# Transposes of four attention steps as 64x64 TensorE tiles, among the tiled products of the step before

## Chip, core and metric

The kernel runs on one core of one Trainium2 chip, in one launch. The metric is the device time of an execution in microseconds (us), taken as the median over several runs; lower is better. The profile describes one of these executions.

## What is computed

The reference is a causal linear attention with decay over blocks of 64 positions, followed by a two-layer network with the tanh form of GELU. Four batches, eight heads, 768 positions, 64 values per head.

```python
for b in range(nb):                      # blocks of 64 positions
    qb, kb, vb = (q[:, :, sl], k[:, :, sl], v[:, :, sl])
    intra = np.einsum('bhic,bhjc->bhij', qb, kb) * Dmask[None]
    intra = np.einsum('bhij,bhjd->bhid', intra, vb)
    inter = np.einsum('bhid,bhde->bhie', qb * lam_pow[None], kv_state)
    out[:, :, sl] = intra + inter
    kb_dec = kb * rev_pow[None]
    kv_state = lam_block[None, :, None, None] * kv_state + np.einsum('bhsd,bhse->bhde', kb_dec, vb)
...
x = attn_out.transpose(0, 2, 1, 3).reshape(B * S, H * D)    # 3072 x 512
h = x @ w_in                                                # 512 x 2048
g = 0.5 * h * (1.0 + np.tanh(c * (h + 0.044715 * h * h * h)))
return g @ w_out                                            # 2048 x 512
```

## The kernel before

**Work units.** Attention is done in 24 steps (`NSTEP`). A step `s` is one stretch of 256 positions of one batch for four of the eight heads; two steps after each other (`s // 2`, the "superblock") cover all heads, and three superblocks make a batch, with a decayed state carried from one to the next. Everything that feeds TensorE is in fp16; PSUM sums are fp32.

**The pieces of a step.**
- `prep(s)`: VectorE scales q by the decay (line 225), ScalarE casts k (line 230), both into one tile `qk16`; POOL scales v (line 215). From step 9 (`FIRST_DMA_T`) on, `prep_qk` also issues a DMA transpose of q and k.
- `stage_t(s)`: for steps 0 to 8 it transposes q and k on TensorE: eight 128x128 transposes (line 246) into one PSUM bank `Tps`, which is then copied to SBUF as `qkT` by ScalarE (steps 1, 5, 6; line 253), by both (2 and 3; lines 250 and 251), or by VectorE (line 255).
- `scores(n)`: 16 matmuls in 64x64 tiles, `Sps` (line 275). `causal(n)` multiplies by the mask on VectorE, giving `PT` (line 284).
- `products(n, s)`: the state products of step n (`OK`, line 310) and the products of `PT` with v for the step before, s (line 324), both in 64x64 tiles; then, for s, two or four products of q with the carried state `u` over the full array (line 333). `x_out` has ScalarE copy the result to `xT` (line 352).
- `update(n, c)`: VectorE carries the state forward (`t`, lines 369 and 372), POOL masks it to `u` (line 379), which line 333 of the next step reads.

A 64x64 tile is a quarter of TensorE's array: a row half, which is the partition half that the operands lie on, and a column half, which is the partition half of PSUM that is written. The list `TILES` gives the order in which matmuls go round the four.

```python
TILES = [(0, 0), (1, 1), (0, 1), (1, 0)]
def half64(i):
    return slice(64 * i, 64 * i + 64)
```

**The network.** `queue_group(g)` puts the matmuls of the two layers for one group of superblocks into a list, `filler`, as small pieces: `mm1` (line 407, `Hps`, with a gelu on ScalarE at line 411), `mm2` (line 422, `O2ps`, copied by ScalarE at line 428), and for later groups `product` (line 476), which works with sums of weights and of activations. `fill(n)` issues the next n pieces. They stand between the pieces of attention, so that TensorE has work while other engines do theirs.

**Order.** `pin` keeps each engine's instructions in the order in which the code issues them. The order around the change is written out by hand at the end of the kernel. `R(n, s)` is `scores(n)`, `products(n, s)`, `causal(n)` and `update(n, 0)`; `U(n)` is `update(n, 1)`. Around steps 5 to 8 (lines 673 to 702):

```python
R(4, None); stage_t(5); U(4); prep(6); fill(2)
R(5, 4); stage_t(6); U(5); prep(7); fill(2)
R(6, 5); U(6); fill(1); prep(8); fill(1)
stage_t(7); fill(2)
R(7, 6); U(7); prep(9); fill(2)
# loop, n = 8:
stage_t(8); prep(10); fill(2); R(8, 7) ...
```

**PSUM.** `Tps`, the two banks of `OK` and the `Hps` and `O2ps` of the network all come from one pool, `ps_M`, of six banks; `Sps` has the other two. Which of the six a tile gets is settled when the kernel is built; a first write waits until the bank's last reader is done.

Of the kernel before, what the change touches and what calls it, by code (L numbers as in the profile page):

```python
# [9 lines left out]
FP16 = mybir.dt.float16  # L10
AF = mybir.ActivationFunctionType
# [4 lines left out]
def kernel(  # L16
# [10 lines left out]
    nc = tc.nc  # L27
    pin = tc.keep_in_program_order
    P = 128
# [9 lines left out]
    FIRST_DMA_T = 9  # L39
# [16 lines left out]
    ps_M = ctx.enter_context(tc.tile_pool(name="psM", bufs=6, space=PSUM))  # L56
# [98 lines left out]
    ident = const.tile([P, P], FP16)  # L155
# [40 lines left out]
    odd(halves[0])  # L196


    a16 = {}
    qkT = {}  # L200

# [18 lines left out]
    def prep_qk(s):  # L220
# [11 lines left out]
        if s >= FIRST_DMA_T:  # L232
# [2 lines left out]
                                            in_=tqk[:].rearrange("p a j h d -> p (a j h d)")))  # L235
            qkT[s] = o

    def stage_t(s):
        if s >= FIRST_DMA_T:
            return  # L240
        tq, tk = a16[s][:2]
        Tps = ps_M.tile([P, 2, 2, 2, P], FP16, tag="M", name="Tps")
        for i, t in enumerate((tq, tk)):
            for hp in range(2):
                for j in range(2):
                    pin(nc.tensor.transpose(Tps[:, i, j, hp, :], t[:, j, 2 * hp : 2 * hp + 2, :],  # L246
                                            ident[:]))
        o = qkp.tile([P, 2, 2, 2, P], FP16, tag="qkT", name=f"qkT_{s}")
        if s in (2, 3):
            pin(nc.scalar.activation(out=o[:, 0], in_=Tps[:, 0], func=AF.Copy))  # L250
            pin(nc.vector.tensor_copy(out=o[:, 1], in_=Tps[:, 1]))
        elif s in (1, 5, 6):
            pin(nc.scalar.activation(out=o[:], in_=Tps[:], func=AF.Copy))
        else:
            pin(nc.vector.tensor_copy(out=o[:], in_=Tps[:]))
        qkT[s] = o

    PTs = {}
    Kps = {}
    xT = {}  # L260
    state = {}
    TILES = [(0, 0), (1, 1), (0, 1), (1, 0)]

    def half64(i):
        return slice(64 * i, 64 * i + 64)

    Ss = {}

    def scores(n):
        o = qkT[n]  # L270
        Sps = ps_S.tile([P, 2, 2, 2, P], FP32, tag="S", name="Sps")
        for hp in range(2):
            for jk in range(2):
                for hl, c in TILES:
                    pin(nc.tensor.matmul(  # L275
                        Sps[half64(c), hl, hp, jk, :], o[half64(hl), 1, jk, hp, half64(c)],
                        o[half64(hl), 0, :, hp, half64(c)], start=True, stop=True,
                        skip_group_check=True))
        Ss[n] = Sps
# [10 lines left out]
    def products(n, s, banks=None, evacuate=True):  # L290


        OK, opened = banks or ([ps_M.tile([P, 512], FP32, tag="M", name=f"OK{c}")
                                for c in range(2)], set())

        def start(c, hl):
            if (c, hl) in opened:
                return False
            opened.add((c, hl))
            return True  # L300

        if n is not None:
            _, tk, tv = a16[n]
            last = (n // 2) % NSB == NSB - 1
            for jk in range(2):
                for hp in range(2):
                    for c, hl in TILES:
                        if c == 1 and last:
                            continue
                        pin(nc.tensor.matmul(  # L310
                            OK[c][half64(hl), 256 + hp * D : 256 + hp * D + D],
                            tk[half64(c), jk, 2 * hp + hl, :], tv[half64(c), jk, 2 * hp + hl, :],
                            start=start(c, hl), stop=(jk == 1), skip_group_check=True))
            Kps[n] = OK
        if s is None:
            return OK, opened
        sbg, half = divmod(s, 2)
        o = qkT.pop(s)
        PT = PTs.pop(s)
        _, _, tv = a16.pop(s)  # L320
        for hp in range(2):
            for jk in range(2):
                for c, hl in TILES:
                    pin(nc.tensor.matmul(  # L324
                        OK[c][half64(hl), hp * P : hp * P + P], tv[half64(c), jk, 2 * hp + hl, :],
                        PT[half64(c), hl, hp, jk, :], start=start(c, hl), stop=False,
                        skip_group_check=True))
        for c in range(2):
            if c == 0 and sbg % NSB == 0:
                continue  # L330
            u = us.pop((s, 0) if c else (s - 2, 1))
            for hp in range(2):
                pin(nc.tensor.matmul(OK[c][:, hp * P : hp * P + P], u[:, hp].rearrange("p l d -> p (l d)"),  # L333
                                     o[:, 0, :, hp, half64(c)], start=False, stop=True,
                                     skip_group_check=True))
        if evacuate:
            x_out(s, OK)
        return OK, opened

    def x_out(s, OK, second=None):  # L340
        sbg, half = divmod(s, 2)
        g, i = group_of[sbg]
        if g not in xT:
            xT[g] = xtp.tile([P, 2, len(groups[g]), 2, SB], FP16, tag="xT", name=f"xT_{g}")
        dst = xT[g][:, half, i]
        for c in range(2):
            d = dst[:, :, c * P : (c + 1) * P].rearrange("p hp (t j) -> p hp j t", j=2)
            o = OK[c][:, 0:256].rearrange("p (hp j t) -> p hp j t", hp=2, j=2)
            if c == 1 and second is not None:
                pin(second.tensor_copy(out=d, in_=o))  # L350
            else:
                pin(nc.scalar.activation(out=d, in_=o, func=AF.Copy))  # L352
# [237 lines left out]
    def R(n, s):  # L590
        if n is not None:
            scores(n)
        products(n, s)
        if n is not None:
            causal(n)
        if s is not None and s % 2 == 1:
            g, i = group_of[s // 2]
            if i == len(groups[g]) - 1 and g > 0:
                queue_group(g)
        if n is not None:  # L600
            update(n, 0)
# [5 lines left out]
    idle(9)  # L607
    prep(0)
    stage_t(0)
    idle(1)  # L610
    square(5)
# [3 lines left out]
    idle(2)  # L615
    R(0, None)
    stage_t(1)
    idle(5)
    U(0)
    prep(2)  # L620
    scores(1)
    products(1, 0)
    causal(1)
    idle(1)
    stage_t(2)
    prep_qk(3)
    update(1, 0)
    update(1, 1, "t")
    idle(3)
    scores(2)  # L630
    products(2, None)
    update(2, 0)
    causal(2)
# [109 lines left out]
```

## Time and profile before

| | |
|---|---|
| Time, median of 4 runs | 205.51 us |
| The four runs | 204.77, 204.85, 206.16, 206.18 us |
| The profiled execution: time, span of its instructions | 204.85 us, 203.1 us |
| TensorE busy, share of the span | 195.8 us, 96% |
| VectorE, ScalarE, POOL busy | 145.0, 108.1, 70.1 us |
| Transposes of steps 5 to 8 on TensorE | 32, first at 42.5 us, last at 55.9 us |
| One such transpose | 219 ns from start to end |
| Granted TensorE clock | 1.00 |

In the profile PE is TensorE's matmuls and PEld its weight loads, DVE is VectorE, ACT is ScalarE. "L246" is line 246 of the kernel, and a row names the tile that is written and the ones that are read. A matmul's duration includes the time that it takes to pass through the array, and matmuls follow each other at a closer distance than that; what each costs in a row of equal ones is read from the distance of their starts, or from the chain, which gives each piece its own share of the time.

### The profile page before, as it was taken

To read this page: it belongs to the slowest core of one execution; us is meant where nothing else is said; L and a number is where in the kernel's file an instruction comes from. 1 tells how busy PE (TensorE), PEld (TensorE's weight loads), DVE (VectorE), ACT (ScalarE), POOL (GpSimd) and SP (SyncE) were. 2 spreads that over 40 slices of the span, in tenths; PEclk is the share of its full clock that TensorE was granted. 3 is DMA by queue.
4 is the path that set the end of the run, shared out by engine and by line. 5 is a ranking of instruction groups with operands and counts; after the bars stand their busy time and mean duration, and the time that the engine had idled before them with its cause. 6 is when DMAs were issued, how large, how long until landed. Compare 5 with 4: busy or idle time off the path is not lost.

```text
span 203.1 us, 5595 instructions
## 1 busy us (share of the span) xinstructions
PE 195.8 (96%) x2325; PEld 127.7 (63%) x2325; DVE 145.0 (71%) x275; ACT 108.1 (53%) x204; POOL 70.1 (35%) x80
## 2 busy tenths in 40 slices
PE   7789999999999999999999999999999999999993
PEld 2456544456875788644688554788554788545882
DVE  4897728777699998929997728996739773136652
ACT  3365778375882573477632477641576431666210
POOL 4695133646586851336135404315412101000000
PEclk9999999999999999999999999999999999999999
DMA  5999999999999999896659992648330003300014
GB/s 157 301 322 391 385 386 377 294 290 326 339 257 230 292 245 147 217 286 165 69 159 235 233 269 80 152 109 134 94 91 0 3 0 103 108 0 0 3 47 160
DMA packets 63937, 37.85 MB, mean 186 GB/s; under 512 B 17576, under 2 KB 59048, under 8 KB 63912
## 3 DMA queue, kind: packets, MB, share of 16 engines
q1 hardware_dynamic: 63616, 37.23, 71.7%
q8 instruction: 18, 0.29, 0.6%
q10 hardware_dynamic: 296, 0.26, 0.4%
q14 instruction: 7, 0.06, 0.1%
HBM read 27.26 MB, written 6.29 MB: 165 GB/s over the span
## 4 chain that ended last, share of the span: by engine, by line
PE 91%; DVE 3%; DMA 1%; POOL 1%; ACT 1%; issue 1%; DVEq 0%
PE Hps L407 37%; PE O2ps L422 10%; PE MB L476 8%; PE MA L476 7%; PE MD L476 7%; PE MC L476 4%; PE Sps L275 4%; PE Hps L522 3%; PE OK L333 3%; PE OK L324 3%; PE Tps L246 2%; DMA lam_in<-in_lam_dram 1%; PE OK L310 1%; DVE PT L284 1%; POOL dq L174 1%
## 5 line engine op out<-in xcount | busy, mean ns | idle before, releaser
L407 PE MATMUL Hps<-xT,w_in 128*128 128x512 f16 (+1 forms) x416 | 79.1, 346 | 0.0
L411 ACT ACTIVATE gT<-Hps 128x512 f16<-128x512 f32 x88 | 52.4, 596 | 22.9 <-PE Hps L407 22.0
L407 PEld LDWEIGHTS <-w_in 128*128 128x128 f16 x416 | 40.3, 98 | 33.5
L379 POOL TENSOR_TENSOR u<-t,lumask 128x256 f16<-128x256 f32 x40 | 31.3, 790 | 79.9 <-DVE t L372 53.1
L452 DVE TENSOR_TENSOR gs<-gT 128x512 f16<-128x512 f16 (+1 forms) x70 | 36.6, 586 | 10.8 <-ACT gT L411 10.6
L284 DVE TENSOR_TENSOR PT<-Sps,mask 128x1024 f16<-128x1024 f32 x24 | 29.2, 1216 | 16.9 <-PE Sps L275 16.8
L476 PEld LDWEIGHTS <-gs 128*128 128x128 f16 x360 | 34.9, 98 | 4.0
L215 POOL TENSOR_TENSOR v<-v,dv 128x512 f16<-128x512 f32 x24 | 29.2, 1220 | 4.4 <-PE O2ps L422 1.8
L352 ACT ACTIVATE xT<-OK 128x256 f16<-128x256 f32 x47 | 18.1, 453 | 19.5 <-PE OK L333 15.9
L422 PE MATMUL O2ps<-w_out,gT 128*128 128x512 f16 x96 | 21.9, 379 | 0.0
L225 DVE TENSOR_TENSOR qk<-q,dq 128x512 f16<-128x512 f32 x23 | 19.2, 835 | 0.0
L230 ACT ACTIVATE qk<-k 128x512 f16<-128x512 f32 x24 | 15.0, 624 | 7.9 <-DMA k<-in_k_dram 7.9
L483 ACT ACTIVATE m<-MB 128x512 f32<-128x512 f32 x9 | 5.4, 597 | 25.4 <-PE MB L476 25.4
L476 PE MATMUL MA<-w_sum,gT 128*128 128x256 f16 x144 | 17.5, 273 | 0.1
L476 PE MATMUL MD<-w_sum,gs 128*128 128x256 f16 x136 | 17.5, 273 | 0.0
L476 PE MATMUL MB<-w_out,gs 128*128 128x256 f16 x144 | 17.2, 273 | 0.0
L476 PEld LDWEIGHTS <-gT 128*128 128x128 f16 x144 | 14.0, 98 | 2.8 <-ACT gT L411 0.3
L422 PEld LDWEIGHTS <-gT 128*128 128x128 f16 x96 | 9.2, 98 | 9.9
L487 DVE TENSOR_TENSOR o<-MA,m 128x512 f32<-128x512 f32 x9 | 6.2, 689 | 12.7 <-ACT m L483 12.7
L372 DVE SCALAR_TENSOR_TENSOR t<-t,lamu,OK 128x64 f32<-128x64 f32 x64 | 14.6, 273 | 0.7
L275 PEld LDWEIGHTS <-qkT 64*64 64x64 f16 x384 | 6.1, 106 | 8.5 <-issue 4.4
L123 DVE TENSOR_TENSOR w_sum<-wo,wo 128x1024 f16<-128x1024 f32 x6 | 7.9, 1363 | 4.2 <-DMA wo<-in_moe_w_out_dram 4.2
(59 smaller groups left out, 167.9 us busy)
## 6 DMA issues: line engine op xcount, KB each, us to landing
q<-in_q_dram SPq DMA_DIRECT2D x24, 256.0 KB, 4.8
k<-in_k_dram SPq DMA_DIRECT2D x24, 256.0 KB, 4.8
v<-in_v_dram SPq DMA_DIRECT2D x24, 256.0 KB, 4.9
out_dram<-o SPq DMA_DIRECT2D x22, 256.0 KB, 4.3
wo<-in_moe_w_out_dram SPq DMA_DIRECT2D x4, 1024.0 KB, 9.4
wi<-in_moe_w_in_dram SPq DMA_DIRECT2D x4, 512.0 KB, 7.4
wi<-in_moe_w_in_dram SPq DMA_DIRECT2D x2, 1024.0 KB, 13.0
out_dram<-o SPq DMA_DIRECT2D x2, 128.0 KB, 1.9
```

The source lines that it names most:

```text
L215: pin(nc.gpsimd.tensor_tensor(wide(tv[:]), ld32[s][2][:], decay(dv, s), ALU.mult))
L225: pin(q_eng.tensor_tensor(wide(tq), q32[:], decay(dq, s), ALU.mult))
L230: pin(nc.scalar.activation(out=wide(tk), in_=k32[:], func=AF.Copy))
L284: pin(nc.vector.tensor_tensor(t[:].rearrange("p a b c d -> p (a b) (c d)"), Ss.pop(n)[:].rearrange("p a b c d -> p (a b) (c d)"), mask[:]. ...
L352: pin(nc.scalar.activation(out=d, in_=o, func=AF.Copy))
L372: pin(nc.vector.scalar_tensor_tensor(t[:, hp, :], state[half][:, hp, :], lamu[:, 2 * half + hp : 2 * half + hp + 1], K[:, hp, :], ALU.mult ...
L379: pin(nc.gpsimd.tensor_tensor(u[:], state[half][:].unsqueeze(2).to_broadcast([P, 2, 2, D]), lumask[:, 2 * half : 2 * half + 2, :].unsqueez ...
L407: pin(nc.tensor.matmul(by_block(Hps[:, i, :]), w_in16[:, c, f * P : (f + 1) * P], x(c), start=(c == 0), stop=(c == NC - 1)))
L411: pin(nc.scalar.activation(out=dst, in_=Hps[:], func=AF.Gelu_apprx_tanh))
L422: pin(nc.tensor.matmul(O2[tau][0][:], gT[:, f % HF, f // HF, tau * P : (tau + 1) * P], w_out16[:, f, :], start=(n == 0), stop=(n == NF - 1)))
L452: pin(nc.vector.tensor_tensor(gsum[m][:, i, :], block(T0, F0, i), block(T1, F1, i), op))
L476: pin(nc.tensor.matmul(dst, lhsT, rhs, start=(i == 0), stop=(i == HF - 1), skip_group_check=True))
```

## The change

The transposes of steps 5 to 8 (`TILED_T`) leave `stage_t`. They are issued inside `products` of the step before, after the tiled products and ahead of the full-array products with `u` (for step 5, whose preceding `products` has no such part, at its end). Each of the eight 128x128 transposes becomes four of 64x64, one on each tile, 32 a step. They are written to two PSUM banks, one for each row half, in place of one. `stage_t` keeps its place and now only copies: two copies of half the size, one from each bank, by ScalarE for steps 5 and 6 and by VectorE for steps 7 and 8. Steps 0 to 4 go as before, and so do the steps from 9 on. `TILES` and `half64` move up unchanged.

```diff
+    TILED_T = range(5, FIRST_DMA_T)
+    Tps = {}
+
+    def transposes(s):
+        tq, tk = a16[s][:2]
+        if s not in TILED_T:
...
+            Tps[s] = t
+            return
+        ts = [ps_M.tile([P, 2, 2, 2, 64], FP16, tag="M", name=f"Tps{c}") for c in range(2)]
+        for i, src in enumerate((tq, tk)):
+            for hp in range(2):
+                for j in range(2):
+                    for c, hl in TILES:
+                        pin(nc.tensor.transpose(ts[c][half64(hl), i, j, hp, :],
+                                                src[half64(c), j, 2 * hp + hl, :],
+                                                ident[half64(c), half64(c)]))
+        Tps[s] = ts
+
     def stage_t(s):
         if s >= FIRST_DMA_T:
             return
-        tq, tk = a16[s][:2]
-        Tps = ps_M.tile([P, 2, 2, 2, P], FP16, tag="M", name="Tps")
-        for i, t in enumerate((tq, tk)):
-            for hp in range(2):
-                for j in range(2):
-                    pin(nc.tensor.transpose(Tps[:, i, j, hp, :], t[:, j, 2 * hp : 2 * hp + 2, :],
-                                            ident[:]))
+        if s not in TILED_T:
+            transposes(s)
+        t = Tps.pop(s)
         o = qkp.tile([P, 2, 2, 2, P], FP16, tag="qkT", name=f"qkT_{s}")
...
-        elif s in (1, 5, 6):
-            pin(nc.scalar.activation(out=o[:], in_=Tps[:], func=AF.Copy))
         else:
-            pin(nc.vector.tensor_copy(out=o[:], in_=Tps[:]))
+            for c in range(2) if s in TILED_T else (None,):
+                src, dst = (t[:], o[:]) if c is None else (
+                    t[c][:].rearrange("p i j h t -> p (i j h) t"),
+                    o[:, :, :, :, half64(c)].rearrange("p i j h t -> p (i j h) t"))
+                if s in (1, 5, 6):
+                    pin(nc.scalar.activation(out=dst, in_=src, func=AF.Copy))
+                else:
+                    pin(nc.vector.tensor_copy(out=dst, in_=src))
         qkT[s] = o
...
         if s is None:
+            if n + 1 in TILED_T:
+                transposes(n + 1)
             return OK, opened
...
+        if n is not None and n + 1 in TILED_T:
+            transposes(n + 1)
         for c in range(2):
             if c == 0 and sbg % NSB == 0:
                 continue
             u = us.pop((s, 0) if c else (s - 2, 1))
```

More of the change, by code (lines that the diff above doesn't have):

```diff
@@ L196, with half64 @@
     odd(halves[0])
+    TILES = [(0, 0), (1, 1), (0, 1), (1, 0)]
+    def half64(i):
+        return slice(64 * i, 64 * i + 64)
     a16 = {}
@@ L236, in prep_qk @@
             qkT[s] = o
+    TILED_T = range(5, FIRST_DMA_T)
[3 more added lines that the diff above has]
+        if s not in TILED_T:
+            t = ps_M.tile([P, 2, 2, 2, P], FP16, tag="M", name="Tps")
+            for i, src in enumerate((tq, tk)):
+                for hp in range(2):
+                    for j in range(2):
+                        pin(nc.tensor.transpose(t[:, i, j, hp, :], src[:, j, 2 * hp : 2 * hp + 2, :],
+                                                ident[:]))
+            Tps[s] = t
+            return
+        ts = [ps_M.tile([P, 2, 2, 2, 64], FP16, tag="M", name=f"Tps{c}") for c in range(2)]
+        for i, src in enumerate((tq, tk)):
+            for hp in range(2):
+                for j in range(2):
+                    for c, hl in TILES:
[3 more added lines that the diff above has]
+        Tps[s] = ts
     def stage_t(s):
@@ L240, in stage_t @@
             return
-        tq, tk = a16[s][:2]
-        Tps = ps_M.tile([P, 2, 2, 2, P], FP16, tag="M", name="Tps")
-        for i, t in enumerate((tq, tk)):
-            for hp in range(2):
-                for j in range(2):
-                    pin(nc.tensor.transpose(Tps[:, i, j, hp, :], t[:, j, 2 * hp : 2 * hp + 2, :],
-                                            ident[:]))
+        if s not in TILED_T:
+            transposes(s)
+        t = Tps.pop(s)
         o = qkp.tile([P, 2, 2, 2, P], FP16, tag="qkT", name=f"qkT_{s}")
         if s in (2, 3):
-            pin(nc.scalar.activation(out=o[:, 0], in_=Tps[:, 0], func=AF.Copy))
-            pin(nc.vector.tensor_copy(out=o[:, 1], in_=Tps[:, 1]))
-        elif s in (1, 5, 6):
-            pin(nc.scalar.activation(out=o[:], in_=Tps[:], func=AF.Copy))
-        else:
-            pin(nc.vector.tensor_copy(out=o[:], in_=Tps[:]))
+            pin(nc.scalar.activation(out=o[:, 0], in_=t[:, 0], func=AF.Copy))
+            pin(nc.vector.tensor_copy(out=o[:, 1], in_=t[:, 1]))
+        else:
+            for c in range(2) if s in TILED_T else (None,):
[6 more added lines that the diff above has]
+                    pin(nc.vector.tensor_copy(out=dst, in_=src))
         qkT[s] = o
@@ L261 @@
     state = {}
-    TILES = [(0, 0), (1, 1), (0, 1), (1, 0)]
-    def half64(i):
-        return slice(64 * i, 64 * i + 64)
     Ss = {}
```

## The prediction

> **What bounds the kernel now.** I read the page first: the busy times of the engines, the span in forty slices, and the shares of the chain that ended last.
>
> ```profile
> PE 195.8 (96%) x2325; PEld 127.7 (63%) x2325; DVE 145.0 (71%) x275; ACT 108.1 (53%) x204; POOL 70.1 (35%) x80
> PE   7789999999999999999999999999999999999993
> PEclk9999999999999999999999999999999999999999
> PE 91%; DVE 3%; DMA 1%; POOL 1%; ACT 1%; issue 1%; DVEq 0%
> ```
>
> TensorE is busy from the fourth slice to the last but one at full granted clock, and the chain is 91% TensorE. Steps 5 to 8 lie at 42 to 59 us, where nothing else bounds. Next I read TensorE's list of waits.
>
> ```profile
> PE idle L584 <- DVE ones L146: 1.5, 1, 1.5
> PE Tps L246 <- POOL dq L174: 0.6, 1, 0.6
> PE Sps L275 <- DVE qkT L251: 0.5, 1, 0.5
> PE OK L324 <- DVE PT L284: 0.4, 1, 0.4
> ```
>
> These waits all fall into the first 17 us. From there on TensorE does one thing after another, so what is taken from its sequence shortens the span one for one, unless the shorter sequence catches up with another engine. Third, the chain in order of time around the change (start, time on the chain, piece):
>
> ```profile
> 42.46 0.12 PE OK L310 x8
> 42.59 0.55 PE Tps L246 x8
> ...
> 45.89 0.45 PE Tps L246 x8
> 46.33 1.73 PE O2ps L422 x8
> 48.06 0.35 PE Sps L275 x16
> 48.41 0.12 PE OK L310 x16
> 48.53 0.23 PE OK L324 x16
> 48.76 0.33 PE OK L333 x4
> ...
> 50.83 0.45 PE Tps L246 x8
> ...
> 55.68 0.45 PE Tps L246 x8
> 56.13 1.75 PE Hps L407 x16
> ```
>
> Every piece of one step can be read here. L246 is the full-array transposes of steps 5, 6, 7 and 8. L275, L310 and L324 are products in 64x64 tiles; L333, L407 and L422 use the full array.
>
> **The change part by part.** *Removed:* four times eight full-array transposes. Three cost 0.45 us each, 56 ns apiece. The first costs 0.55, because it stands behind tiled work and carries the switch from tiles to the full array, 0.10; step 4's products have no L333 behind them. That switch stays, and is paid by the L422 that now follows. So 4 x 0.45 = 1.80 us leave.
>
> *Added:* four times 32 transposes of 64x64, at the end of the tiled products of the step before. The trace has no tiled transpose. The nearest row is L310: the same tile, the same 64 moving columns, a 64-column weight load from the same qk tile before each, and two output banks split by row tile, as the change does. Its 16 take 0.12 us, 7.5 ns each, so 32 take 0.24. That is my value: 4 x 0.24 = 0.96 us. Bounds from the rows: below, the work can't be less than nothing, so the gain is at most the 1.80 removed; above, the tiles don't overlap at all for transposes. Then each 64-column transpose takes half of L246's 56 ns, 28 ns, and 32 take 0.90 us, 3.58 in all, a loss of 1.8. I stay at the L310 row, since only the transpose flag and the fp16 output differ from it.
>
> *Switches of mode:* none is added or saved. The new transposes stand behind L324 (L310 in step 4) and ahead of L333, inside a stretch that is tiled already. In the old place they stood between full-array work. The sum on TensorE is 0.96 - 1.80 = -0.84 us.
>
> A rule speaks against this. The Trainium skill, TensorE: Matmul & The Clock Gate, section on the 56 ns that aren't 53.3, says that matmul starts are never closer than about 25 ns however few the columns. By it 32 transposes would take an estimated 0.80 us, and the change would lose 4 x 0.35 = 1.4 us. The L310 row, at 7.5 ns from start to start over four tiles, says that this floor doesn't hold across tiles, and I go by the row.
>
> **Who might now be late.** The program's order is kept on each engine, so I went through every wait that moved.
>
> Inputs: the transposes of a step now need its q and k earlier. They stand on TensorE ahead of L333 and all filler, so a late k would stop everything. For step 6 q is done at 44.73 and k at 44.78, and the transposes come at about 45.15. For step 7 k is the closest.
>
> ```profile
> 45.81 0.77 ACT L352 ACTIVATE xT<-OK 128x256 f16<-128x256 f32 x2 [0.55 <-PE OK L333]
> 46.43 1.02 ACT L253 ACTIVATE qkT<-Tps 128x1024 f16<-128x1024 f16 x1
> 47.35 0.62 ACT L230 ACTIVATE qk<-k 128x512 f16<-128x512 f32 x1
> ```
>
> That is the timeline of ScalarE (start, time). In step 5's products L333 comes after the new 0.24, but 0.21 was saved before it, so it starts about 0.04 later, and so do these three. The evacuation of step 6 becomes two halves. A half is 0.60 us (L250, 597 ns), the second starting about 0.48 after the first as the two-in-a-row L428 do, so both take 1.08 instead of 1.02. It ends at about 47.57, and k of step 7 at 48.07. TensorE wants that qkT for scores(6) at 47.99 - 2 x 0.21 = 47.57: the half microsecond of slack that stood there is used up, and I book a wait of 0.03 us (0 to 0.15). The first k transpose of step 7 comes at about 48.30, after 48.07.
>
> Steps 7 and 8 are evacuated by VectorE, two halves of 0.42 (L251, 420 ns) for one of 0.69, 0.15 us more for each. After step 7's VectorE was idle for 1.42 us, waiting for scores. For step 8 the halves need no wait for a TensorE that just finished, and end near 56.3; scores(8) come near 57.0. If that cover were gone, each would cost at most its 0.15.
>
> L333 itself waits for u from POOL: u of step 4 is done at 45.19 and of step 5 at 47.94, ahead of 45.55 and 48.6. No DMA is issued or moved by the edit; loads, output stores and DMA transposes keep their place in SP's queue.
>
> Banks: the pool has six, and two instead of one are held from the products of step n until the evacuation ahead of step n+1's scores. In the built program the banks that transposes 5 to 8 and the products behind them take were last read, at the latest, by the gelu of the first L407 block (ends 52.25, wanted at about 52.9) and by the evacuation of the transposes before (about 47.5, wanted at 48.2). None is late. From step 9 on the sequence of tenants is the old one with other numbers. If one of these came late, it would cost the missing part of one 0.6 us activation.
>
> Sum: -0.84 + 0.03 = -0.81 us, say 0.8. All TensorE work after 58 us moves up by that, and since its only other gap there is 0.2 us at 76 us, it stays. The profiled run has a span of 203.1 in a time of 204.85: 202.3 and 204.05 after. The runs shown are 204.77, 204.85, 206.16 and 206.18, with median 205.51; the profiled run is one of the low pair. I forecast the median: 205.51 - 0.8 = 204.7 us.
>
> **The rivals.** (a) *Slower: the tiles don't overlap for transposes.* Place: the 32 transposes of each step. Price: 0.90 - 0.45 = 0.45 us a step, 1.8 us over four; scores(6) come later by more than qkT of step 6 does, so no wait adds to it. Time 207.3. It decides from 14 ns per transpose up (0.45 / 32), where the gain is gone; over 1% needs 30 ns, for example if each transpose also drained its tile. For it: no row shows a tiled transpose, nor two kinds of pass overlapping. Against it: L310 and L275 overlap fourfold, and L246 stands beside L333 and L407 with no gap, so the transpose flag alone costs no drain.
>
> (b) *The gain is eaten by waits.* ScalarE's chain of x, qkT and k in step 6 comes late by more than I booked, for example 0.5 us by one more activation ahead of it, and one bank comes late. Time 205.3. For it: the slack is nearly nothing. Against it: it occurs once, in step 6; from step 7 on there is half a microsecond or more.
>
> (c) *The transposes vanish under their neighbours.* If the tiled passes fill gaps between L310 and L324, up to 1.8 us is saved: 203.7, still under 1%. Against it: the tiled stretch has no gap to fill but its switches.
>
> **How the numbers follow.** Forecast 0.62, at 204.7; (b) 0.15; (a) 0.18, about half of it above 1%, with still slower transposes in its tail; (c) 0.05. One per cent is 2.05 us, about what a measurement of this kernel can tell from no change. The forecast, (b) and (c) lie within it; faster by over 1% needs more than the whole 1.80 that is removed, and can come only from the scatter of the runs or something that I don't see: 0.06. Slower by over 1%: 0.13, from the upper half of (a) and its tail. Within: 0.81. The likeliest case alone spans 203.9 to 205.4, since runs differ by 1.4 among themselves. The range reaches from (c) with some scatter, 203.3, to just short of (a), 206.8.
>
> **What would show it.** Right: each step's transposes stand on the chain with 0.24 us in place of 0.45, behind L324 and ahead of L333; the old places show filler following filler; scores(8), at 57.80 before, start near 57.0; TensorE's waits after 21 us show at most one for qkT of step 6, below 0.15. Wrong: tiled transposes with 28 ns or more from start to start mean rival (a); a TensorE wait for ScalarE's qkT or for k at 47 to 49 us means (b); scores(8) early but the span unchanged means that the gain was given back after 58 us, which I have excluded.

## The result, and the profile after

| | before | changed |
|---|---|---|
| Median time | 205.18 us (58 runs, 204.76 to 206.43) | 206.22 us (37 runs, 204.66 to 207.59) |
| Ratio | | 1.0038, 95% interval 1.0024 to 1.0053 |
| Profiled execution: time, span | 204.85, 203.1 us | 206.31, 204.5 us |
| TensorE instructions (weight loads and matmuls) | 4650 | 4842 |

The change made the kernel slower by 0.4%; the ratio is that of the means, the medians differ by 0.5%. The forecast was 204.7 us, 0.4% below the median of 205.51 that it started from. First the page of the changed kernel: the busy times, the fetches of instructions over DMA, and the shares of the chain that ended last.

```profile
PE 194.6 (95%) x2421; PEld 126.9 (62%) x2421; DVE 145.3 (71%) x277; ACT 108.2 (53%) x206; POOL 70.0 (34%) x80
q8 instruction: 19, 0.31, 0.7%
PE 89%; DVE 4%; issue 2%; DMA 1%; POOL 1%; ACT 1%; DVEq 0%
```

TensorE's busy time fell by 1.2 us and the span grew by 1.4. The share called "issue", time for which the profile shows no cause, went from 1% to 2%. The instruction row of the page before was:

```profile
q8 instruction: 18, 0.29, 0.6%
```

TensorE's list of waits from 20 us to 200 us was empty before. Now it reads:

```profile
PE Tps L263 <- issue: 1.4, 1, 1.4
PE Hps L437 <- issue: 0.5, 1, 0.5
```

The chain in order of time shows where they lie (L301, L336, L352, L363, L437 and L452 are the old L275, L310, L324, L333, L407 and L422; L263 is the tiled transposes):

```profile
48.14 0.23 PE OK L352 x16
48.36 0.18 PE Tps L263 x22
48.54 1.37 issue
49.91 0.28 PE Tps L263 x10
50.19 0.33 PE OK L363 x4
...
54.48 0.23 PE OK L352 x16
54.70 0.28 PE Tps L263 x32
54.98 0.22 PE OK L363 x2
55.20 0.44 PE Hps L437 x4
55.63 0.47 issue
56.11 3.22 PE Hps L437 x28
```

Step 8's 32 tiled transposes cost 0.28 us, against 0.45 for eight full ones. So the tiles overlap. But in step 7 TensorE stops for 1.4 us behind the 22nd transpose, with neither q nor k nor a bank beginning there, and once more in the middle of a row of filler matmuls that wait for nothing.

**What stops it.** The page's instruction queue q8 carried 18 packets before and 19 now, each of 16 KB. 4842 instructions in 0.31 MB are 64 bytes each, so a packet is a block of 256. The weight loads (PEld) around the two stops:

```profile
48.12 0.31 PEld L263 LDWEIGHTS <-qk 64*64 64x64 f16 x23
49.91 0.17 PEld L263 LDWEIGHTS <-qk 64*64 64x64 f16 x9 [1.48 <-issue]
54.98 0.48 PEld L437 LDWEIGHTS <-w_in 128*128 128x128 f16 x5
56.11 0.97 PEld L437 LDWEIGHTS <-w_in 128*128 128x128 f16 x9 [0.65 <-issue]
```

Each matmul has its weight load ahead of it, so the n-th weight load of the trace is number 2n - 1 of TensorE's stream and the n-th matmul number 2n. The first weight load behind the first stop is number 1217, the first behind the second 1473 (matmuls 1216 and 1472 are recorded as starting with them): the stops are 256 instructions apart, the length of a block. The trace's packet records show the two fetches; the first packet of a profile is taken as the block behind number 449, the next as that behind 705, and so on. The first ran from 47.25 to 48.44 us, and TensorE, whose last matmul had started at 48.35, went on at 49.91. The second ran from 53.82 to 54.85; TensorE's last matmul had started at 55.36, and it went on at 56.11. From start to start, beyond the usual spacing, the two stops are 1.56 and 0.64 us.

The Trainium skill, Runtime: NRT & Kernel Launch, section Instruction fetch mechanics, describes the same: instructions reach an engine in 16 KB blocks of 256, each fetched by the sequencer's own DMA while it works through the one before, and crossing an edge is mostly hidden. The blocks agree with the packets here. "Mostly hidden" agrees with the other edges of this profile, at which TensorE doesn't stop, and not with these two, at 1.56 and 0.64 us.

**The balance.** scores(8) began at 57.80 us before and at 59.25 now, 1.45 later:

```profile
57.80 0.42 PE L275 MATMUL Sps<-qkT 64*64 64x128 f16 x16
59.25 0.42 PE L301 MATMUL Sps<-qkT 64*64 64x128 f16 x16
```

The two stops are 2.20; without them scores(8) would be 0.75 earlier. Forecast was 0.81. From there on the two traces run alike, to spans that differ by 1.4.

*Theory F* (supply): a block of 256 instructions is used up faster than the next arrives. The change adds 48 TensorE instructions a step (32 transposes for 8, each with its weight load) where they were densest already. From its first matmul to its last ahead of the edge, the block ahead of 1217 took 7.2 us before and 3.4 now, the one ahead of 1473 8.2 and 5.5. *Theory W* (the rival): the early transposes wait for data or a bank, and the profile fails to name it.

### The profile page after: what moved, and what is told of

It reads as the page before. It is cut to its first block, busy times and chain, and to the rows that moved or that the text cites. A ratio compares the mean times of both kernels' runs of the same rounds, so it can differ in the third digit from the quotient of the medians.

```text
span 204.5 us, 5790 instructions
## 1 busy us (share of the span) xinstructions
PE 194.6 (95%) x2421; PEld 126.9 (62%) x2421; DVE 145.3 (71%) x277; ACT 108.2 (53%) x206; POOL 70.0 (34%) x80
## 4 chain that ended last, share of the span: by engine, by line
PE 89%; DVE 4%; issue 2%; DMA 1%; POOL 1%; ACT 1%; DVEq 0%
PE Hps L437 37%; PE O2ps L452 10%; PE MB L506 8%; PE MA L506 7%; PE MD L506 7%; PE MC L506 4%; PE Sps L301 4%; PE Hps L552 3%; PE OK L363 3%; PE OK L352 3%; DMA lam_in<-in_lam_dram 1%; PE OK L336 1%; DVE PT L310 1%; POOL dq L174 1%; PE Tps L254 1%
## 5 line engine op out<-in xcount | busy, mean ns | idle before, releaser
L437 PE MATMUL Hps<-xT,w_in 128*128 128x512 f16 (+1 forms) x416 | 78.9, 346 | 0.5 <-issue 0.5
L437 PEld LDWEIGHTS <-w_in 128*128 128x128 f16 x416 | 40.3, 98 | 34.1 <-issue 0.6
L310 DVE TENSOR_TENSOR PT<-Sps,mask 128x1024 f16<-128x1024 f32 x24 | 29.2, 1216 | 16.7 <-PE Sps L301 16.7
L452 PE MATMUL O2ps<-w_out,gT 128*128 128x512 f16 x96 | 21.9, 379 | 0.0
L230 DVE TENSOR_TENSOR qk<-q,dq 128x512 f16<-128x512 f32 x23 | 19.2, 837 | 0.0
L235 ACT ACTIVATE qk<-k 128x512 f16<-128x512 f32 x24 | 15.0, 625 | 7.3 <-DMA k<-in_k_dram 7.3
L452 PEld LDWEIGHTS <-gT 128*128 128x128 f16 x96 | 9.1, 98 | 10.0
L301 PEld LDWEIGHTS <-qkT 64*64 64x64 f16 x384 | 6.2, 106 | 8.5 <-issue 4.2
```

What stands on the lines that cost most here:

```text
L230: pin(q_eng.tensor_tensor(wide(tq), q32[:], decay(dq, s), ALU.mult))
L235: pin(nc.scalar.activation(out=wide(tk), in_=k32[:], func=AF.Copy))
L310: pin(nc.vector.tensor_tensor(t[:].rearrange("p a b c d -> p (a b) (c d)"), Ss.pop(n)[:].rearrange("p a b c d -> p (a b) (c d)"), mask[:]. ...
L437: pin(nc.tensor.matmul(by_block(Hps[:, i, :]), w_in16[:, c, f * P : (f + 1) * P], x(c), start=(c == 0), stop=(c == NC - 1)))
L452: pin(nc.tensor.matmul(O2[tau][0][:], gT[:, f % HF, f // HF, tau * P : (tau + 1) * P], w_out16[:, f, :], start=(n == 0), stop=(n == NF - 1)))
```

## The experiments

All numbers of blocks and edges are counted as above. An edge has the number of the first instruction behind it; the block "ahead of" it ends there, and the block that belongs to it begins there. "Lands" is the end of the fetch packet of the block that begins at the edge.

**e1: the edges moved.**

```diff
+            w = P if to_split[0] > 0 else 512     # to_split = [16]
+            to_split[0] -= 1
+            for i in range(0, 512, w):
+                pin(nc.tensor.matmul(t[:, i : i + w], ones[:, 0:P], ones[:, 0:w], start=True, stop=True))
-            pin(nc.tensor.matmul(t[:], ones[:, 0:P], ones[:], start=True, stop=True))
```

> The changed kernel, with the first 16 of the 512-column idle matmuls at the start cut into four of 128 columns each: the same columns, 96 more TensorE instructions (48 matmuls with their weight loads) ahead of everything, and nothing else. Theory F (TensorE's instructions arrive in blocks of 256, and a block isn't there in time when the one before it is used up too fast): the waits without a cause stand at the same numbers of TensorE's stream, 1217 and 1473, and so at 48 matmuls earlier in the code: inside the tiled state products (L336) of R(6, 5) in place of step 7's transposes, and inside the PT products (L352) of R(7, 6) in place of the first filler after them; perhaps one more at 1729, in the filler after R(8, 7). By the costs of the pieces the block before 1217 now lasts 5.2 us and not 3.3, so the first wait is shorter than 1.4 us, 0 to 0.8; all together 0.3 to 1.8 us; time 204.3 to 206. Theory W (the early transposes wait for data or for a bank that the profile fails to name): the wait stays inside the transposes of step 7, behind the 22nd, with about 1.4 us, and the time stays near 206.2.

Measured: 205.23 us, ratio 0.9994 (0.9969 to 1.0020). No wait at 1217, whose block landed 2.3 us ahead. One at 1473, 1.75 us by starts, inside the PT products of R(7, 6), as theory F placed it. TensorE's timeline (start, time, and in brackets the idle time before):

```profile
53.84 0.28 PE L352 MATMUL OK<-PT,v 64*64 64x128 f16 x6
55.67 0.35 PE L352 MATMUL OK<-PT,v 64*64 64x128 f16 x10 [1.55 <-issue]
```

The wait left the transposes and went to products that the change doesn't touch, by the distance that the stream was moved. Theory W falls in the form in which the transposes wait. The total, 1.75 us, is at the top of what was expected: the block landed at 54.12, 5.1 us after its predecessor's first instruction. The profiled run took 206.98 us and was the slowest of the twelve, so the others need not have had a stop of this length.

**e2: fuller blocks without tiled transposes.** In the kernel before, around steps 5 to 8:

```diff
-                pin(nc.tensor.matmul(O2[tau][0][:], gT[...], w_out16[:, f, :], ...))
+                w = P if narrow[0] else DM        # L407's matmuls likewise
+                for e in range(0, DM, w):
+                    pin(nc.tensor.matmul(O2[tau][0][:, e : e + w], gT[...], w_out16[:, f, e : e + w], ...))
```

> The kernel before, all transposes over the full array and in their old place, but with the filler matmuls from ahead of R(4) to R(7, 6) cut into pieces of 128 columns: 216 more TensorE instructions for the same columns (about 0.25 us more of TensorE time by 56 ns for 128 columns against 216 ns for 512), so that the blocks ahead of stream numbers 1217 and 1473 last 3.7 and 5.3 us by the costs of the pieces, about as in the changed kernel (3.3 and 5.5), where the kernel before had 7.2 and 8.3. Theory F: waits without a cause appear at 1217 (inside the PT products of R(6, 5)) and at 1473, 0.5 to 2 us together, and the time is 205.8 to 207.3. Theory W: no new wait, 205.2 to 205.6.

Measured: 205.38 us, ratio 1.0004 (0.9985 to 1.0023); no wait after 20 us. Theory F's expectation missed, and the time is what W expected. The blocks did pass in 3.8 and 5.3 us, but the fetches were quicker: they landed 2.1 and 2.8 us after the first instruction of the block before, against 3.5 and 4.9 in the changed kernel, and so 1.75 and 2.5 us ahead. Passing a block in 3.8 us isn't enough by itself; the fetch has to be slow too. e9 repeats the test with a denser stream.

**e3: half the instructions.**

```diff
-                    for c, hl in TILES:
-                        pin(nc.tensor.transpose(ts[c][half64(hl), i, j, hp, :],
-                                                src[half64(c), j, 2 * hp + hl, :], ...))
+                    for c in range(2):
+                        pin(nc.tensor.transpose(ts[c][:, i, j, hp, :],
+                                                src[half64(c), j, 2 * hp : 2 * hp + 2, :], ...))
```

> The changed kernel with 16 transposes of 64 rows by 128 columns a step in place of 32 of 64 by 64: the same place, the same two banks, the same columns, half the instructions. Theory F: the block ahead of stream number 1217 lasts 7.3 us by the costs of the pieces, the one ahead of 1473 5.0, so the wait in step 7's transposes is gone and 0 to 1 us may be left at 1473; the gain of the tiles stays, less one more switch of mode a step (0.1 us): 204.4 to 205.6. Theory W: transposes and banks stand as early as in the changed kernel, the wait of 1.4 us in step 7 stays: about 206.3.

Measured: 205.20 us, ratio 0.9995 (0.9968 to 1.0022). As theory F expected, no stop at an edge: the block ahead of 1217 lasted 7.3 us. The build gave the banks to other tenants, though, and the tiled transposes now do wait for one. The whole list of waits after 20 us:

```profile
PE Tps L263 <- ACT gT L441: 0.5, 1, 0.5
PE Tps L254 <- DVE qk L230: 0.2, 1, 0.2
PE OK L336 <- ACT o L458: 0.2, 1, 0.2
```

So a wait for a bank or for data looks different: the profile names it.

**e4: less DMA traffic.**

```diff
     def load_ahead(s):
         if s < NSTEP:
-            load_step(s)
+            ld32[s] = ld32[5 + (s - 9) % 4]
```

> The changed kernel without the loads of q, k and v from step 9 on (these steps compute with the values of steps 5 to 8): less DMA traffic from about 45 us on. TensorE's instruction stream is as in the changed kernel. Theory F, with the fetch of a block slowed by the data's DMA traffic: the fetches at 47 and 54 us start sooner after they are due, and the waits at 1217 and 1473 shrink, from 1.8 us to 0 to 0.9 together; time 203 to 205. If the fetch doesn't depend on that traffic, the waits stay at 1.4 and 0.5. Theory W: waits unchanged.

Measured: 205.38 us, ratio 0.9997 (0.9970 to 1.0024), above the range that I gave. The wait stands behind the same 22nd transpose, with the same stream, and is far shorter (0.18 us of idle time in the brackets against 1.37); at 1473 there is none.

```profile
49.34 0.36 PE L263 MATMUL Tps<-ident,qk 64*64 64x64 f16 x22
49.88 0.28 PE L263 MATMUL Tps<-ident,qk 64*64 64x64 f16 x10 [0.18 <-issue]
```

The fetches landed 2.3 and 2.8 us after the first instruction of the block before. The order of data and banks is unchanged, which speaks for the fetch. By itself this doesn't exclude theory W, since the other loads may also have landed sooner.

**e5: the changed kernel again**, as it is.

> The changed kernel as it is, beside the next three on the same chip. Theory F: waits without a cause at stream numbers 1217 (behind the 22nd transpose of step 7) and 1473 (in the filler after R(7, 6)), of another length than before, since the fetches start at other times: 0.3 to 2.5 us together; elsewhere none; time 205.2 to 206.8. Theory W: the wait in step 7's transposes again, with 1.4 us.

Measured: 205.66 us, ratio 1.0002 (0.9980 to 1.0023). The stop in step 7 came at the same instruction with 1.2 us by starts; none at 1473, where the block landed 1.7 us ahead. The length differs from run to run with the fetch. On this chip the loss in time isn't resolved.

**e6 and e11: a version with longer blocks.**

```diff
-    TILED_T = range(5, FIRST_DMA_T)
+    TILED_T = (5, 6, 8)
```

> The changed kernel with TILED_T = (5, 6, 8): step 7's transposes over the full array, in their old place. By the costs of the pieces the blocks ahead of stream numbers 1217, 1473 and 1729 last 5.6, 6.0 and 7.2 us, against 3.3, 5.5 and 9.5 in the changed kernel. Theory F: at most one short wait there (0 to 0.5 us), three fifths of a microsecond gained (three steps of 0.19): 204.5 to 205.4, below the kernel before on the same chip by 0.3 to 0.6. Theory W, with the wait in step 7's transposes alone: the same time. Theory W with a wait for every tiled transpose: three quarters of the loss stays.

> The kernel of e6_tiled_5_6_8 again, for a closer interval and a second profile. Theory F: no wait at 1217, 1473 and 1729, or one below 0.5 us; the ratio to the kernel before between 0.996 and 1.000.

Measured: 205.42 us, ratio 0.9986 (0.9963 to 1.0009), and 205.36 us, ratio 0.9992 (0.9967 to 1.0016). Theory F gave 204.5 to 205.4 for e6 and 0.3 to 0.6 below the kernel before; its median came out at the top of that and 0.14 below the 205.56 of the kernel before, a smaller gain. The form of theory W in which step 7 alone waits gave the same time, so this run doesn't separate the two. Neither profile has a stop at an edge; at 1217, 1473 and 1729 the blocks landed 2.6 us ahead or more. The chain of e6 around the place where the changed kernel stopped (L254 is the full-array transposes, the old L246):

```profile
48.12 0.23 PE OK L352 x16
48.35 0.33 PE OK L363 x4
48.68 0.86 PE O2ps L452 x4
49.54 0.87 PE Hps L437 x8
50.41 0.45 PE Tps L254 x8
```

Its profiled span is 202.5, 0.6 below the 203.1 of before, as three steps of 0.19 give. But it was the fastest of its twelve runs; the span of e11, the same kernel, was 203.3, with TensorE waiting 0.4 us there for step 4's q. Steps 5 and 6 still have their early tiled transposes and two banks without a wait.

**e7: more of the same instructions.**

```diff
-        for i, src in enumerate((tq, tk)):
+        for i, src in 2 * ((0, tq), (1, tk)):
```

> The changed kernel with each tiled transpose of steps 5 to 8 issued twice, into the same place: 256 more TensorE instructions, which cost four times 0.26 us of TensorE's time, 1.0 us. By the costs of the pieces the blocks ahead of stream numbers 1217, 1473 and 1729 last 4.6, 3.7 and 2.9 us. Theory F: waits without a cause at all three numbers, wherever they fall in the code (scores of step 7, filler after it), 2.4 to 7 us together, time 208.5 to 213. Theory W: 1.0 us more than the changed kernel, about 207.2, and no new place of waiting.

Measured: 208.32 us, ratio 1.0136 (1.0096 to 1.0176); the profiled run, 207.41, was the fastest of the six. Its stops lie at 1473 and 1729, in plain filler, 0.73 and 1.54 us by starts; at 1217 the block came in time.

```profile
54.45 0.74 PE L263 MATMUL Tps<-ident,qk 64*64 64x64 f16 x64
55.12 0.29 PE L363 MATMUL OK<-qkT,u 128*128 128x128 f16 x2
55.25 0.60 PE L437 MATMUL Hps<-xT,w_in 128*128 128x256 f16 x4
57.22 1.03 PE L437 MATMUL Hps<-xT,w_in 128*128 128x256 f16 x8 [1.38 <-issue]
```

The 64 transposes pass without a gap, and the stop comes where their block ends. The median is a little under the range for F, and 1.1 us over the 207.2 for W. The stops, at 2.3 us, are just below the 2.4 to 7 that I expected, and come at two of the three numbers.

**e8: the same stream with less DMA traffic.** The edits of e4 and e7 together.

> As e7_twice, and without the loads of q, k and v from step 9 on (these steps compute with the values of steps 5 to 8). The stream of TensorE's instructions is the same as in e7_twice. If the fetch of a block is slowed by the data's DMA traffic, the waits at 1217, 1473 and 1729 are shorter than in e7_twice by a third or more and the time is lower by 1 to 3 us. If the fetch takes its time anyway, waits and time are as in e7_twice within 0.7 us.

Measured: 206.58 us, ratio 1.0043 (1.0017 to 1.0069): 1.7 us below e7 beside it. The stops at 1473 and 1729 went from 0.73 and 1.54 to 0 and 0.25 us; their blocks landed 2.0 and 1.8 us after the first instruction of the block before, against 3.2 and 3.3. This profile has another stop of 1.1 us at edge 449, at 17.45 us, ahead of anything that the edit touches.

**e9: the dense stream without any tiled transpose.** To e2's edits:

```diff
-        for hp in range(2):
+        for hp in 3 * (0, 1) if n in (4, 5, 6, 7, 8) else (0, 1):     # in scores(n)
```

> The kernel before, all transposes over the full array and in their old place, with the narrow filler of e2_before_narrow and the 16 score matmuls of steps 4 to 8 issued three times over into the same place: 536 more TensorE instructions, and 5 x 2 x 0.25 + 0.25 = 2.75 us more of TensorE's time, so 208.3 without any wait. By the costs of the pieces the blocks ahead of stream numbers 1217, 1473 and 1729 last 4.3, 3.9 and 3.9 us. Theory F: waits without a cause at these numbers, which all fall into filler matmuls here, with no tiled transpose anywhere, 0.5 to 5 us together; each ends 1.2 to 1.6 us after its block has landed; time 208.8 to 213. Theory W: no such wait, 208.3.

Measured: 209.06 us, ratio 1.0176 (1.0142 to 1.0209), in F's range and 0.8 over W's 208.3. The profiled run stopped at all three edges, all in filler: 0.17 us at 1217, 0.90 at 1473, 1.17 at 1729. The chain at 1473 (L410 is the old L407):

```profile
51.64 0.56 PE Hps L410 x10
52.20 0.73 issue
52.94 0.49 PE Hps L410 x6
```

At 1729 the list of waits names something:

```profile
PE Hps L410 <- ACT xT L352: 1.0, 1, 1.0
```

The x that it names was done at 57.62 and TensorE went on at 58.03; block 1729 had landed at 56.59, 1.44 before. Where a named wait holds TensorE elsewhere in these profiles, it goes on at most 0.06 us after the instruction named has ended, as at 54.67 us in e3. So x can have held it until 57.67 here, and only the last 0.36 of the 1.17 us must be the edge's. The stops at 1217 and 1473 have no such rival. They come without tiled transposes, without early transposes and with one bank. This carries theory F where e2 didn't.

**e10: two tiled steps, edges moved.** `TILED_T = (5, 8)`, and e1's edit with 7 in place of 16.

> The changed kernel with TILED_T = (5, 8) and the first 7 idle matmuls at the start cut into four: by the costs of the pieces the blocks ahead of stream numbers 1217, 1473 and 1729 last 6.2, 6.2 and 7.0 us. Theory F: no wait at these numbers, two times 0.19 us gained against the kernel before: 0.4 us below it on this chip, ratio 0.998. Theory W with a wait for each tiled transpose: half of the changed kernel's loss, ratio 1.002.

Measured: 204.84 us, ratio 0.9986 (0.9959 to 1.0013); no stop at an edge. Theory F gave 0.998; theory W with a wait for each tiled transpose gave 1.002, which lies outside the interval. In its profiled run TensorE waited 0.6 us at 41 us for q of step 4, a wait that has nothing to do with the edges.

**e12: the kernel before, one look.**

> The kernel before again, one look. Its times fall into two groups, near 204.9 and near 206.1. Theory F: a run of the upper group has a wait of about 1.2 us at stream number 449, at 16 to 18 us, where the profiled run of the lower group had its block 1.35 us ahead, the least of all blocks; a run of the lower group has none there.

Measured: 204.78 us, of the lower group; no stop, block 449 in 1.8 us ahead. It doesn't show what the upper group is.

**All the stops together.** Every stop at an edge, in us: the block's landing, TensorE's last start before it, its next start, and the difference of landing and next start.

| run | edge | lands | last start | goes on | after landing |
|---|---|---|---|---|---|
| changed | 1217 | 48.44 | 48.35 | 49.91 | 1.47 |
| changed | 1473 | 54.85 | 55.36 | 56.11 | 1.26 |
| e1 | 1473 | 54.12 | 53.90 | 55.67 | 1.55 |
| e4 | 1217 | 48.36 | 49.52 | 49.88 | 1.52 |
| e5 | 1217 | 49.20 | 49.27 | 50.48 | 1.28 |
| e7 | 1473 | 51.39 | 51.84 | 52.67 | 1.28 |
| e7 | 1729 | 55.93 | 55.57 | 57.22 | 1.29 |
| e8 | 449 | 17.08 | 17.45 | 18.55 | 1.47 |
| e8 | 1729 | 55.47 | 56.57 | 56.92 | 1.45 |
| e9 | 1217 | 46.54 | 47.89 | 48.11 | 1.57 |
| e9 | 1473 | 51.42 | 51.98 | 52.94 | 1.52 |
| e9 | 1729 | 56.59 | 56.81 | 58.03 | 1.44 |

Whatever the code at the edge, TensorE goes on 1.26 to 1.57 us after the landing (at 1729 in e9 x may have had a part in it). At the edges from 449 to 1985 of all profiles it stopped wherever the block had landed 1.15 us ahead or less, and nowhere where it had landed 1.75 us ahead or more; of seven between, one stopped, for 0.17 us.

**What stays open.** How much of the 0.4% is these stops can't be summed from profiles, since their length changes from run to run: 2.2 us in one profile of the changed kernel, 1.2 in another. The first of these runs, at 206.31 us, is near the median, 206.22; on the chip of the second the loss didn't show. What sets the start of a fetch isn't shown: at 1473 in e1 it began 3.8 us after the first instruction of the block before, at 1729 in e8 0.9 us. That data traffic slows the fetch is supported by e4 against the changed kernel and by e8 against e7, but leaving out loads also changes other timing, and e2 had quick fetches with all loads. No version here is shown to beat the kernel before: the intervals of e6, e10 and e11 all contain 1.

## Why the prediction was wrong

*What bounds the kernel:* right about TensorE, as a sequence with no waits after 17 us. But I read "nothing else bounds" from engines, banks and DMA loads, and left out the supply of TensorE's own instructions.

*The cost of 32 tiled transposes:* 0.24 us predicted from L310, 0.28 measured in step 8. Each step gained about 0.19 us on TensorE, against 0.21: scores(6) came at 47.58 in place of 47.99 with two steps changed, and scores(4) had already come 0.03 earlier.

```profile
47.99 0.42 PE L275 MATMUL Sps<-qkT 64*64 64x128 f16 x16
47.58 0.43 PE L301 MATMUL Sps<-qkT 64*64 64x128 f16 x16
```

The floor of 25 ns between starts (the Trainium skill, TensorE: Matmul & The Clock Gate, section on the 56 ns that aren't 53.3), which I set aside on the strength of L310, doesn't hold across the tiles: 0.28 / 32 is 8.8 ns.

*Switches of mode:* right, none added: the eight L452 behind step 5's transposes take 1.83 us on the chain where eight L422 took 1.73, the 0.10 that was to move there. *ScalarE's chain in step 6:* right within 0.1 us. Two of its three lines (L284 and L235 are the old L253 and L230), beside those shown of before:

```profile
46.46 1.08 ACT L284 ACTIVATE qkT<-Tps 128x512 f16<-128x512 f16 x2
47.40 0.65 ACT L235 ACTIVATE qk<-k 128x512 f16<-128x512 f32 x1
```

Two halves take 1.08 us as worked out, k of step 7 is done at 48.05 (47.40 + 0.65; I had 48.07), and scores(6) came at 47.58 without the 0.03 of waiting that I booked. Banks and POOL's u: right, no wait.

*The step that failed* is "Who might now be late". It says "I went through every wait that moved", and it went through data and banks alone. The sum of 128 instructions that replace 32 was made in time and never in instructions: with their weight loads 192 more, most of a block, in 13 us. The number stood on the page, as x2325 and as 18 packets of instructions. With it the blocks could have been laid over the chain: 256 instructions in 3.4 us, where no block after the first 20 us had taken less than 7.2. The trace of before also held a size for the fetch: blocks landed up to 4.9 us after the first instruction of their predecessor (the one behind edge 705: 21.56 us against 16.70), so a block used up in 3.4 us could leave TensorE dry for 1.5.

*The rivals:* (a) fell, the tiles overlap. (b) had the right outcome, a gain eaten by a wait, with the wrong wait and too small a price; the place it named, 47 to 49 us, was near the stop only by chance. (c) fell.

## What to carry to other kernels

Cutting matmuls into tiles divides their time and multiplies their instructions. Before adding many short instructions to a dense stretch, count the engine's instructions between one block edge and the next, and compare the time in which 256 of them pass with the time that earlier blocks took from the first instruction of their predecessor to landing, and 1.6 us on top. An "issue" wait in the middle of equal matmuls that wait for nothing is worth counting: see whether its instruction number falls on the edges. What removed such waits here was fewer instructions in the block ahead (e3, e6).

## What the runs showed of the hardware

A stop at an edge ends 1.26 to 1.57 us after the fetch packet has ended, 12 times out of 12, the one at 1729 in e9 perhaps with another cause beside it. The packet itself took 0.9 to 1.4 us at these stops. For the blocks ahead of 1217, 1473 and 1729, the time from the first instruction of one to the landing of the next varied from -0.2 to 5.1 us with all loads in place. Whether this is why runs of one kernel differ by a microsecond or two isn't shown: the kernel before differs by 1.7 among its runs, and neither of its profiles, both of runs below 204.9, has a stop.
